# Attention and expert layer in one kernel: squares of the first two key blocks summed by VectorE, loads and splits of the first expert weights tied to later jobs, token operands of two chunks made by GpSimd

## The chip, the cores and the metric

The kernel runs on one core of a Trainium2 chip. The metric is the device time of one execution in microseconds (us). The engines are PE (TensorE), DVE (VectorE), ACT (ScalarE), POOL (GpSimd) and SP (SyncE, which only issues DMAs here). Each engine takes its own instructions in order and waits on semaphores for the others.

## What is computed

Random-feature attention, and on its result a mixture of eight experts, all in float32:

```python
proj = einsum('bhsd,md->bhsm', x, omega); sq = sum(x*x, -1) / 2   # x = q or k, scaled
phi  = exp(h - max(h)) / sqrt(m),  h = proj - sq
num  = phi(q) @ (phi(k)^T v);  den = phi(q) @ sum_s phi(k)        # B 4, H 8, S 576, D 64, m 128
x    = (num / (den + 1e-6)) as [2304, 512]
P    = exp(x @ w_gate - max), 8 rounds of row and column scaling
out += P[:, e:e+1] * (relu(x @ w1[e]) @ w2[e])                     # 8 experts, 512 -> 1024 -> 512
```

## The kernel before

**Attention, 36 jobs.** A job is one half (four heads, two rows of each partition) of a block of k or q; job 4 and job 21 are the leftover k rows ("kr"), 22 and 35 the leftover q rows ("qr"). Jobs 0 to 3 are k, from 5 on k and q take turns, from 31 on only q. A block of 512 KB serves two jobs that follow each other (0 and 1, 2 and 3; from job 5 on every second one, such as 5 and 7).

Each block is loaded (`load`) and its squares are summed (`squares`, L281): ACT squares 1024 numbers a partition into `sq`, POOL halves them three times (L290), DVE sums the last eight of each row (L292, `sqs`). Each job (`feature_stages`, L304) transposes on PE (L311, `tp`), copies to `th` (ACT for k, DVE for q), multiplies with omega (L324, `pp`), and DVE takes two maxima (L327, `mx`), the small shift `cn` (L331, L332: two inputs in SBUF) and `ex`; ACT does the exponentials (L339, L342). A k job then adds to `kv` on PE; a q job transposes, multiplies with `kvs`, and its result goes to `xf`.

**Operands.** When six token tiles of `xf` are complete (a chunk; three in all: chunk 0 is complete as job 21 begins, chunk 1 at job 34, chunk 2 after the last job), `token_operands` (L99) makes seven operand tiles: up to one DVE subtraction each on `xf` (L110, four in all), an ACT cast (L125), a DVE subtraction (L126), and a 768 KB store (L128). There are four `xs` buffers for all of it; chunk 2's tiles are used by the first matmuls (L539) straight away.

**Expert weights.** `stage` (L170) loads 1 MB of w1 or w2 in two DMAs of 512 KB to `st`, `split` (L180) makes one of seven high and low parts: up to one POOL operation on `st` or `t` (L186), an ACT cast `wh` (L216), and for the first w1 a POOL subtraction `wl` (L217). After the attention 16 units of 1/16 of the expert weights run, bound by matmuls.

**What sets the order.** The Python loop over the jobs (L740) names what may be done when, but a scheduler that plays the program through with a timeline of its own then sets each engine's order: what has no dependency is drawn forward. So the loads of `st`, written at jobs 6 and 24, stand on SP between the first loads of q and k. DMAs are numbered round eight semaphores, so that one waits for the eighth before it.

Of the kernel before, what the change touches and what calls it, by code (L numbers as in the profile page):

```python
# [9 lines left out]
F32 = mybir.dt.float32  # L10
F32R = mybir.dt.float32r
AF = mybir.ActivationFunctionType
ALU = mybir.AluOpType
# [3 lines left out]
def raw(ap):  # L17

    return ap.bitcast(F32)
# [3 lines left out]
def moe_attention_kernel(  # L23
# [23 lines left out]
    nc = tc.nc  # L47
    B, H, S, D = q.shape
# [4 lines left out]
    P = 128  # L53
# [26 lines left out]
    def bank(name):  # L80
        return ps[0].tile([P, 512], F32, tag="b", name=name)
# [9 lines left out]
    ORDER = [1, 5, 6, 3, 7, 2, 4]  # L91
# [4 lines left out]
    def token_tile():  # L96
        return xs.tile([P, 2, 2, HL], F32R, tag="xs", bufs=XSB, name="xs")

    def token_operands(c, x):  # L99

        def q(r, h):
            h = 1 - h
            return x[:, 2 * r : 2 * r + 2, h * HL : (h + 1) * HL]

        last = c == NCH - 1
        gate_steps = logits(c, x)
        next(gate_steps)

        def sub(o, a, b):
            nc.vector.tensor_tensor(o, a, b, op=ALU.subtract)  # L110

        for i in ORDER:
            if i == 5:
                sub(q(0, 0), q(0, 1), q(0, 0))
            elif i == 6:
                sub(q(0, 0), q(1, 1), q(0, 0))
            elif i == 7:
                sub(q(0, 1), q(1, 1), q(0, 1))  # L120
            elif i == 4:
                sub(q(0, 0), q(1, 0), q(0, 0))
            o = {3: q(1, 1), 7: q(0, 1), 2: q(1, 0)}.get(i, q(0, 0))
            t = token_tile()
            nc.scalar.copy(t[:, 0], o)  # L125
            nc.vector.tensor_tensor(t[:, 1], o, raw(t[:, 0]), op=ALU.subtract)  # L126
            xdram[c, i] = xd.tile([P, 2, 2, HL], F32, name=f"xd{c}_{i}")
            nc.sync.dma_start(out=xdram[c, i], in_=raw(t))  # L128
            if last:
                xop[0, c, i] = t  # L130
                first(0, c, i, 0)
                first(0, c, i, 1)
            next(gate_steps, None)
            yield
# [31 lines left out]
    wst, wt = {}, {}  # L166
    tmp = {}

    def stage(u, w):
        e, fb = units[u]  # L170
        f0 = fb * FB * P
        for r in range(2):
            wst[u, w, r] = t = wp.tile([P, 2, 2, HD], F32, tag="st", bufs=4, name="st")
            if w == 1:
                src = w1[e][r * HD : (r + 1) * HD, f0 : f0 + FB * P]
            else:
                src = w2[e][f0 + r * HD : f0 + (r + 1) * HD, :]
            nc.sync.dma_start(out=t.rearrange("p k h c -> p k (h c)"), in_=src.rearrange("(k p) c -> p k c", p=P))

    def split(u, w, i):  # L180

        def q(r, h):
            return wst[u, w, r][:, :, 1 - h if w == 1 else h]

        def tt(o, a, b, op=ALU.subtract):
            nc.gpsimd.tensor_tensor(o, a, b, op=op)  # L186


        if w == 1:

            if i == 5:
                tmp[u] = wp.tile([P, 2, HD], F32, tag="t", bufs=1, name="t")
                tt(tmp[u], q(0, 1), q(1, 1), ALU.add)
            elif i == 6:
                tt(tmp[u], tmp[u], q(0, 0))
            elif i == 3:
                tt(tmp[u], q(1, 0), tmp[u])
            elif i == 7:
                tt(q(0, 1), q(0, 0), q(0, 1))
            o = {1: q(0, 0), 7: q(0, 1), 2: q(1, 0), 4: q(1, 1)}[i] if i not in (5, 6, 3) else tmp[u]  # L200
        else:

            if i == 5:
                tt(q(0, 0), q(0, 1), q(0, 0))
            elif i == 6:
                tt(q(0, 0), q(0, 0), q(1, 1))
            elif i == 7:
                tt(q(0, 1), q(1, 1), q(0, 1))
            elif i == 4:
                tt(q(0, 0), q(1, 0), q(0, 0), ALU.add)  # L210
            o = {3: q(1, 1), 7: q(0, 1), 2: q(1, 0)}.get(i, q(0, 0))
        pool = wp if w == 1 else op_
        bufs = 7 * w
        hi = pool.tile([P, 2, HD], F32R, tag=f"w{w}h", bufs=bufs, name="wh")
        lo = pool.tile([P, 2, HD], F32R, tag=f"w{w}l", bufs=bufs, name="wl")
        nc.scalar.copy(hi, o)  # L216
        (nc.vector if u > 0 or (w == 2 and i in (1, 6, 7, 4)) else nc.gpsimd).tensor_tensor(lo, o, raw(hi), op=ALU.subtract)  # L217
        wt[u, w, i] = (hi, lo)
# [3 lines left out]
    sc = sc_cm.__enter__()  # L222
# [54 lines left out]
    sqt = {}  # L277
# [3 lines left out]
    def squares(which, key):  # L281

        t = rawt[which, key]
        n = 1 if key[0] == "r" else 2
        s = sc.tile([P, H, n, D], F32, tag="sq", bufs=2, name="sq")
        nc.scalar.activation(s, t[:, :H], AF.Square, scale=1.0 / math.sqrt(2.0 * math.sqrt(D)))
        w = D
        while w > 8:
            w //= 2
            nc.gpsimd.tensor_tensor(s[..., :w], s[..., :w], s[..., w : 2 * w], op=ALU.add)  # L290
        o = sc.tile([P, H, n], F32, tag="sqs", bufs=6, name="sqs")
        nc.vector.tensor_reduce(o, s[..., :w], axis=AX.X, op=ALU.add)  # L292
        sqt[which, key] = o

# [9 lines left out]
    def feature_stages(which, key, hh, on_act):  # L304


        tin = rawt[which, key].rearrange("p h j d -> p (h j d)")
        tp = bank("tp")
        for i in range(4):
            o = (4 * hh + i) * P  # L310
            nc.tensor.transpose(tp[:, i * P : (i + 1) * P], tin[:, o : o + P], ident)  # L311
        th = sc.tile([P, 4, P], F32, tag="th", bufs=2, name="th")
        if which == "k":
            nc.scalar.copy(th.rearrange("p a s -> p (a s)"), tp)
        else:
            nc.vector.tensor_copy(th.rearrange("p a s -> p (a s)"), tp)
        yield
        sq = sqt[which, key].rearrange("p h j -> p (h j)")
        mx = sc.tile([P, 4, 2], F32, tag="mx", bufs=4, name="mx")
        pp = [bank("pp") for _ in range(2)]  # L320
        for i in range(4):
            for g in range(2):
                r = slice(g * D, (g + 1) * D)
                nc.tensor.matmul(pp[g][:, i * M : (i + 1) * M], lhsT=th[r, i], rhs=omt[r], start=True, stop=True)  # L324
        p3 = [p.rearrange("p (h m) -> p h m", h=4) for p in pp]
        for g in range(2):
            nc.vector.reduce_max(mx[:, :, g], p3[g], axis=AX.X)  # L327

        s8 = sq[:, 8 * hh : 8 * hh + 8]
        cn = sc.tile([P, 8], F32, tag="cn", bufs=4, name="cn")  # L330
        nc.vector.tensor_tensor(cn, s8, mx.rearrange("p h g -> p (h g)"), op=ALU.subtract)  # L331
        nc.vector.tensor_tensor(cn, cn, s8, op=ALU.subtract)  # L332
        res = []
        for g in range(2):
            ex = sc.tile([P, 4, M], F32, tag="ex", bufs=8, name="ex")
            c4 = cn[:, g::2]
            if on_act and g == 1:
                for i in range(4):
                    nc.scalar.activation(ex[:, i, :], p3[g][:, i, :], AF.Exp, bias=c4[:, i : i + 1])  # L339
            else:  # L340
                nc.vector.tensor_tensor(ex, p3[g], c4.unsqueeze(2).to_broadcast([P, 4, M]), op=ALU.add)
                nc.scalar.activation(ex, ex, AF.Exp)  # L342
            res.append(ex)
        yield
        yield
        return res
# [369 lines left out]

    def ensure_loads(i):
        for it in list(need):
            if it[0] <= (i if it[1] == "v" else i + 2):
                need.remove(it)  # L720
                load(it[1], it[2])
                if it[1] != "v":
                    sq_todo.append(it)
        while sq_todo and sq_todo[0][0] <= i + 1:
            _, w, key = sq_todo.pop(0)
            squares(w, key)

    sq_todo = []
    active = []

    def tick():
        for it in list(active):
            jb, gen = it
            try:
                next(gen)
            except StopIteration:
                active.remove(it)

    ensure_loads(0)
    for i, jb in enumerate(jobs):  # L740
        if i == 4:
            prepare_gate()
        if i == 6:
            stage(0, 1)
        if i >= 8 and i % 2 == 0 and (i - 8) // 2 < 7:
            split(0, 1, ORDER[(i - 8) // 2])
        if i == 24:
            stage(0, 2)
        gen = k_job(jb[1], jb[2]) if jb[0] == "k" else q_job(*jb[1:])
        active.append((jb, gen))  # L750
        tick()
        ensure_loads(i + 1)
# [90 lines left out]
```

## Time and profile before

| | us |
|---|---|
| three runs: median (lowest to highest) | 1651.64 (1648.07 to 1652.31) |
| the profiled execution: its time, its span | 1651.03, 1649.1 |
| PE busy | 1589.7 (96%) |
| DVE, ACT, POOL busy | 1397.0, 778.0, 272.2 |

The profiled execution lies 0.61 us below the median and has 1.9 us around its span. A busy PE is not PE at its best: PE, DVE and ACT can each be busy while another sets the pace.

### The profile page before, as it was taken

Reading aid. Unit: us, or ns where it says so; the run is one execution under the profiler, and the core shown is the slowest. Engines: PE = TensorE matmul, PEld = TensorE weight load, DVE = VectorE, ACT = ScalarE, POOL = GpSimd, SP = SyncE. Lnnn points to the kernel's source line nnn. Section 1 sums busy time; section 2 is a strip of 40 time slices with the busy share of each in tenths; the row PEclk is TensorE's granted clock in tenths of the full one; section 3 lists DMA queues with packets and bytes.
Section 4 is the critical chain, followed back from the end, with each engine's and each line's share of the span. In section 5 each row is a group of like instructions: output and inputs, shape, how many; then the busy total and the mean of one; then the engine's idle time right before and its main releaser. Section 6 shows DMA issues by size and latency. Waiting matters only on the chain.

```text
span 1649.1 us, 31431 instructions
## 1 busy us (share of the span) xinstructions
PE 1589.7 (96%) x12318; PEld 1555.0 (94%) x12318; DVE 1397.0 (85%) x2771; ACT 778.0 (47%) x1396; POOL 272.2 (17%) x236
## 2 busy tenths in 40 slices
PE   5898889999999999999999999999999999999998
PEld 4777689999999999999999999999999999999997
DVE  4698889898979898889888898989898888889877
ACT  5687755444434343443544443444444444444333
POOL 6421041111102011111111110102111111101003
PEclk8799999999999999999999999999999999999999
DMA  9332576665665656566657565665665665655562
GB/s 232 110 110 110 213 284 234 204 229 170 237 201 200 216 200 212 202 218 217 218 177 257 168 220 202 216 210 206 210 217 207 217 216 185 218 185 192 175 227 78
DMA packets 105314, 329.79 MB, mean 200 GB/s; under 512 B 14800, under 2 KB 43984, under 8 KB 105168
## 3 DMA queue, kind: packets, MB, share of 16 engines
q1 hardware_dynamic: 105168, 327.79, 58.4%
q8 instruction: 98, 1.61, 0.4%
q14 instruction: 48, 0.39, 0.1%
HBM read 306.53 MB, written 21.23 MB: 199 GB/s over the span
## 4 chain that ended last, share of the span: by engine, by line
PE 83%; DVE 10%; POOL 2%; DMA 1%; issue 1%; ACT 1%; SPq 1%; DVEq 0%; ACTq 0%; POOLq 0%
PE hx L539 23%; PE x L640 22%; PE hz L539 17%; PE z L640 11%; PE w L640 5%; PE pp L324 2%; DVE out L666 2%; DVE sm L576 2%; DVE mx L327 1%; DVE bl L576 1%; POOL sq L290 1%; DVE wl L217 1%; PE np L425 1%; PE kv L351 1%; DVE sl L615 1%
## 5 line engine op out<-in xcount | busy, mean ns | idle before, releaser
L539 PE MATMUL hx<-xs,wh 128*128 128x384 f32 x1536 | 374.0, 337 | 1.9 <-ACT xs L125 1.3
L666 DVE SCALAR_TENSOR_TENSOR out<-x,prob,out 128x256 f32<-128x256 f32 x497 | 233.6, 476 | 65.6 <-PE x L640 64.2
L539 PE MATMUL hz<-xs,wh 128*128 128x384 f32 x1152 | 281.8, 336 | 1.7 <-ACT xs L125 1.0
L539 PEld LDWEIGHTS hx<-xs,wh 128*128 128x128 f32 x1536 | 269.7, 188 | 3.7 <-ACT xs L125 2.4
L186 POOL TENSOR_TENSOR st<-st 128x512 f32<-128x512 f32 x80 | 132.0, 1651 | 728.0 <-DVE wl L217 725.4
L539 PEld LDWEIGHTS hz<-xs,wh 128*128 128x128 f32 x1152 | 202.2, 188 | 3.2 <-ACT xs L125 1.8
L539 PE MATMUL hx<-xs,wl 128*128 128x384 f32 x768 | 199.2, 336 | 0.0
L618 ACT ACTIVATE bh<-hr 128x512 fp32r<-128x512 f32 x144 | 91.2, 634 | 222.8 <-PE x L640 217.9
L666 DVE SCALAR_TENSOR_TENSOR out<-z,prob,out 128x256 f32<-128x256 f32 x252 | 120.2, 477 | 57.9 <-PE z L640 57.1
L216 ACT CAST wh<-st 128x512 fp32r<-128x512 f32 x176 | 104.7, 620 | 110.6 <-PE hx L539 45.1
L614 ACT CAST sh<-sm 128x512 fp32r<-128x512 f32 x144 | 89.7, 623 | 139.3 <-PE z L640 99.7
L539 PE MATMUL hz<-xs,wl 128*128 128x384 f32 x576 | 150.1, 335 | 0.0
L539 PEld LDWEIGHTS hx<-xs,wl 128*128 128x128 f32 x768 | 138.7, 188 | 0.0
L576 DVE SCALAR_TENSOR_TENSOR sm<-hr,sm 128x256 f32<-128x256 f32 x288 | 133.7, 464 | 2.7
L217 DVE TENSOR_TENSOR wl<-st,wh 128x512 fp32r<-128x512 f32 x169 | 119.6, 719 | 13.1 <-ACT wh L216 12.8
L576 DVE SCALAR_TENSOR_TENSOR bl<-hr,bh 128x512 fp32r<-128x512 f32 x144 | 118.5, 823 | 2.5 <-ACT bh L618 2.5
L640 PE MATMUL z<-wh,sh 128*128 128x256 f32 x576 | 117.9, 281 | 2.8 <-ACT sh L597 2.7
L640 PE MATMUL x<-wh,sh 128*128 128x256 f32 x576 | 117.6, 284 | 0.7 <-DVE out L666 0.6
L640 PE MATMUL x<-wl,sh 128*128 128x256 f32 x576 | 118.3, 281 | 0.0
L588 ACT ACTIVATE ah<-hr 128x256 fp32r<-128x256 f32 x144 | 60.3, 419 | 122.1 <-PE x L640 98.9
L640 PE MATMUL z<-wh,sl 128*128 128x256 f32 x576 | 115.5, 282 | 1.6 <-DVE sl L598 1.6
L640 PE MATMUL z<-wl,sh 128*128 128x256 f32 x576 | 116.8, 281 | 0.0
(150 smaller groups left out, 3470.1 us busy)
## 6 DMA issues: line engine op xcount, KB each, us to landing
xs<-xd SPq DMA_DIRECT2D x329, 768.0 KB, 4.4
st<-in_moe_w_dram SPq DMA_DIRECT2D x64, 512.0 KB, 4.9
xd<-xs SPq DMA_DIRECT2D x21, 768.0 KB, 4.6
k<-in_k_dram SPq DMA_DIRECT2D x8, 512.0 KB, 4.8
v<-in_v_dram SPq DMA_DIRECT2D x8, 512.0 KB, 5.4
q<-in_q_dram SPq DMA_DIRECT2D x8, 512.0 KB, 4.2
out_dram<-out SPq DMA_DIRECT2D x32, 128.0 KB, 1.9
kr<-in_k_dram SPq DMA_DIRECT2D x4, 128.0 KB, 5.4
```

The costliest lines, as they stand in the source:

```text
L186: nc.gpsimd.tensor_tensor(o, a, b, op=op)
L216: nc.scalar.copy(hi, o)
L217: (nc.vector if u > 0 or (w == 2 and i in (1, 6, 7, 4)) else nc.gpsimd).tensor_tensor(lo, o, raw(hi), op=ALU.subtract)
L290: nc.gpsimd.tensor_tensor(s[..., :w], s[..., :w], s[..., w : 2 * w], op=ALU.add)
L324: nc.tensor.matmul(pp[g][:, i * M : (i + 1) * M], lhsT=th[r, i], rhs=omt[r], start=True, stop=True)
L539: nc.tensor.matmul(pb, lhsT=a[:, k, g * P : (g + 1) * P], rhs=x[:, b, k, :], start=i in (1, 5, 2) and j == 0, stop=j == len(prods) - 1, sk ...
L576: nc.vector.scalar_tensor_tensor(o, in0=a, scalar=0.0, in1=b, op0=ALU.max, op1=op)
L588: nc.scalar.activation(ah, a11, AF.Relu)
L614: nc.scalar.copy(sh, sm)
L618: nc.scalar.activation(bh, a[:, 1:], AF.Relu)
L640: nc.tensor.matmul(pb, lhsT=ops[s][i][a][:, f], rhs=wt[u, 2, i][b][:, f], start=bool(start) and j == 0, stop=j == len(prods) - 1, skip_gro ...
L666: nc.vector.scalar_tensor_tensor(o, in0=pb, scalar=p, in1=o, op0=ALU.mult, op1=ALU.add)
```

## The change

Six edits. (1) The first two blocks' squares (k of jobs 0 to 3) are no longer halved by POOL: DVE sums all 64 of each row. (2) `th` of those jobs is copied by DVE and not ACT. (3) Before the loads of the first w1 and w2, POOL copies eight numbers of the newest `cn` into the buffer, so that the load waits for that job. (4) The first w1 is loaded at job 10 and split from job 14 on. (5) Loads of k and q are named three jobs ahead (two before), squares two ahead (one before), with eight `sqs` buffers. (6) Both subtractions of an operand go to POOL for chunks 0 and 1.

```diff
+        eng = nc.vector if last else nc.gpsimd
         def sub(o, a, b):
-            nc.vector.tensor_tensor(o, a, b, op=ALU.subtract)
+            eng.tensor_tensor(o, a, b, op=ALU.subtract)
...
-            nc.vector.tensor_tensor(t[:, 1], o, raw(t[:, 0]), op=ALU.subtract)
+            eng.tensor_tensor(t[:, 1], o, raw(t[:, 0]), op=ALU.subtract)
...
             wst[u, w, r] = t = wp.tile([P, 2, 2, HD], F32, tag="st", bufs=4, name="st")
+            if u == 0:
+                nc.gpsimd.tensor_copy(t[:, 0, 0, :8], last_cn[-1])
...
-        while w > 8:
+        early = len(sqt) < 2
+        while w > 8 and not early:
...
-        if which == "k":
+        if which == "k" and len(sqt) > 4:
             nc.scalar.copy(th.rearrange("p a s -> p (a s)"), tp)
...
-            if it[0] <= (i if it[1] == "v" else i + 2):
+            if it[0] <= (i if it[1] == "v" else i + 3):
...
-        while sq_todo and sq_todo[0][0] <= i + 1:
+        while sq_todo and sq_todo[0][0] <= i + 2:
...
-        if i == 6:
+        if i == 10:
             stage(0, 1)
-        if i >= 8 and i % 2 == 0 and (i - 8) // 2 < 7:
-            split(0, 1, ORDER[(i - 8) // 2])
+        if i >= 14 and i % 2 == 0 and (i - 14) // 2 < 7:
+            split(0, 1, ORDER[(i - 14) // 2])
```

On DVE, before, job 3 (its maxima are `mx_283`) and job 4 (`mx_340`); `sqs_483` and `sqs_562` are the sums of the k block of jobs 9 and 11 and the q block of jobs 10 and 12:

```order
L327 TENSOR_REDUCE mx_283<-pp_285 128x4
L331 TENSOR_TENSOR cn_296<-sqs_122,mx_283 128x8
L332 TENSOR_TENSOR cn_296<-cn_296,sqs_122 128x8
L341 TENSOR_TENSOR ex_299<-pp_284,cn_296 128x512
L292 TENSOR_REDUCE sqs_483<-sq_478 128x16
L292 TENSOR_REDUCE sqs_562<-sq_557 128x16
L327 TENSOR_REDUCE mx_340<-pp_341 128x4
```

The same place in the changed kernel, where job 3's maxima are `mx_284`, job 4's `mx_334`, and the sums of those two blocks `sqs_421` and `sqs_480`:

```order
L349 TENSOR_TENSOR ex_237<-pp_222,cn_234 128x512
L299 TENSOR_REDUCE sqs_421<-sq_416 128x16
L299 TENSOR_REDUCE sqs_480<-sq_475 128x16
L334 TENSOR_REDUCE mx_284<-pp_285 128x4
L334 TENSOR_REDUCE mx_284<-pp_286 128x4
L338 TENSOR_TENSOR cn_297<-sqs_109,mx_284 128x8
L339 TENSOR_TENSOR cn_297<-cn_297,sqs_109 128x8
L349 TENSOR_TENSOR ex_300<-pp_285,cn_297 128x512
L299 TENSOR_REDUCE sqs_682<-sq_677 128x16
L299 TENSOR_REDUCE sqs_734<-sq_729 128x16
L334 TENSOR_REDUCE mx_334<-pp_335 128x4
```

Both pairs of sums now stand one job earlier; further on the sum for the k block of jobs 17 and 19 moves from in front of job 8's maxima to job 7's, and the three after it (a q block, kr, qr) all stand in front of job 9's.

On ACT in the changed kernel, from job 8's second exponential (`ex_580`) to job 10's (`ex_714`); `wh` are the casts of the first w1, which stood between jobs 1 and 4 before:

```order
L350 ACTIVATE ex_580<-ex_580 128x512
L292 ACTIVATE sq_1288<-qr_1231 128x512
L222 CAST wh_867<-st_597 128x512
L222 CAST wh_1014<-t_1012 128x512
L415 COPY qt_689<-qp_684 128x512
L347 ACTIVATE ex_663<-pp_646,cn_657 128x128 x4
L415 COPY qt_696<-qp_691 128x512
L350 ACTIVATE ex_660<-ex_660 128x512
L222 CAST wh_1148<-t_1012 128x512
L321 COPY th_727<-tp_722 128x512
L347 ACTIVATE ex_717<-pp_700,cn_711 128x128 x4
L350 ACTIVATE ex_714<-ex_714 128x512
```

Two casts now stand in front of job 9's exponentials and a third in front of job 11's `th`; the other four follow before job 11's exponentials.

On POOL in the changed kernel, chunk 0's operands (`xs`, `xf`), with the two copies that hold the load of the first w2:

```order
L128 TENSOR_TENSOR xs<-xf,xs 128x768
L112 TENSOR_TENSOR xf<-xf 128x2x384 x2
L128 TENSOR_TENSOR xs<-xf,xs 128x768
L179 COPY st<-cn 128x8 x2
L112 TENSOR_TENSOR xf<-xf 128x2x384
L372 TENSOR_TENSOR kvs<-kvs 128x4 x2
L128 TENSOR_TENSOR xs<-xf,xs 128x768 x3
L112 TENSOR_TENSOR xf<-xf 128x2x384
L128 TENSOR_TENSOR xs<-xf,xs 128x768
L192 TENSOR_TENSOR t<-st 128x512
L128 TENSOR_TENSOR xs<-xf,xs 128x768
L192 TENSOR_TENSOR st<-st 128x2x256
```

These eleven `xs` and `xf` subtractions stood on DVE between jobs 20 and 24; chunk 1's eleven moved in the same way.

## Rows read from the trace of the kernel before

**Rows 1.** Busy time by stage: PE, PEld, DVE, ACT, POOL, clock, DMA share, GB/s.

```profile
0.00:20.00 20.00, 10.31 (x96) 8.21 (x97) 6.44 (x14) 9.82 (x17) 11.39 (x26) 1.00 1.00 249
80.00:110.00 30.00, 28.42 (x504) 25.43 (x503) 27.56 (x73) 25.59 (x63) 10.10 (x15) 1.00 0.33 91
110.00:135.00 25.00, 21.67 (x322) 17.65 (x317) 23.02 (x51) 20.25 (x47) 3.38 (x5) 0.93 0.60 228
245.00:1649.00 1404.00, 1391.59 (x9847) 1383.51 (x9845) 1214.22 (x2377) 615.34 (x1033) 190.67 (x126) 1.00 0.60 204
```

**Rows 2.** Waits of DVE, 0 to 80 us: total, times, longest.

```profile
DVE sqs L292 <- POOL sq L290: 27.0, 8, 9.4
```

**Rows 3.** Timeline, DVE and POOL: start, length, what, idle before.

```profile
37.09 0.29 DVE L292 TENSOR_REDUCE sqs<-sq 128x16 f32<-128x128 f32 x1 [6.65 <-POOL sq L290]
38.93 1.28 DVE L327 TENSOR_REDUCE mx<-pp 128x4 f32<-128x512 f32 x2
...
47.37 1.28 DVE L327 TENSOR_REDUCE mx<-pp 128x4 f32<-128x512 f32 x2
95.55 2.64 POOL L290 TENSOR_TENSOR sq<-sq 128x512 f32<-128x512 f32 x3 [8.14 <-ACT sq L286]
```

**Rows 4.** Timeline, early loads on SP and a square.

```profile
13.96 2.25 SPq L178 DMA_DIRECT2D st<-in_moe_w_dram  x2
18.01 6.20 SPq L263 DMA_DIRECT2D qr<-in_q_dram  x2
24.32 0.56 SPq L274 DMA_DIRECT2D k<-in_k_dram  x1
30.44 1.06 ACT L286 ACTIVATE sq<-k 128x1024 f32<-128x1024 f32 x1 [3.02 <-DMA k<-in_k_dram]
```

**Rows 5.** Timeline, DVE's small `cn` beside POOL, and without.

```profile
22.59 0.93 DVE L331 TENSOR_TENSOR cn<-sqs,mx 128x8 f32<-128x8 f32 x1
23.46 1.26 POOL L186 TENSOR_TENSOR t<-st 128x512 f32<-128x512 f32 x1
23.56 1.18 DVE L332 TENSOR_TENSOR cn<-cn,sqs 128x8 f32<-128x8 f32 x1
29.34 0.17 DVE L331 TENSOR_TENSOR cn<-sqs,mx 128x8 f32<-128x8 f32 x1
```

**Rows 6.** Timeline, one k block from its load to its sum, and job 9.

```profile
52.65 0.37 SPq L274 DMA_DIRECT2D k<-in_k_dram  x1
56.66 1.06 ACT L286 ACTIVATE sq<-k 128x1024 f32<-128x1024 f32 x1 [1.31 <-DMA k<-in_k_dram]
61.10 0.27 DVE L292 TENSOR_REDUCE sqs<-sq 128x16 f32<-128x128 f32 x1
67.76 1.28 DVE L327 TENSOR_REDUCE mx<-pp 128x4 f32<-128x512 f32 x2
```

**Rows 7.** Timeline, a cast of the first w1 on ACT.

```profile
24.75 0.62 ACT L216 CAST wh<-t 128x512 fp32r<-128x512 f32 x1 [2.60 <-POOL t L186]
```

**Rows 8.** Groups to 245 us: count, busy, mean ns, idle before.

```profile
L126 DVE TENSOR_TENSOR xs<-xf,xs 128x768 fp32r<-128x768 f32 x21 | 19.7, 952 | 6.1 <-ACT xs L125 5.9
L125 ACT CAST xs<-xf 128x768 fp32r<-128x768 f32 x21 | 17.1, 840 | 4.6 <-DMA xd<-xs 2.6 <-DVE xf L110 1.7 <-DVE xs L126 0.3
L110 DVE TENSOR_TENSOR xf<-xf 128x768 f32<-128x768 f32 x12 | 11.4, 950 | 0.0
L290 POOL TENSOR_TENSOR sq<-sq 128x256 f32<-128x256 f32 x20 | 14.5, 728 | 2.0 <-ACT sq L286 1.3
L217 POOL TENSOR_TENSOR wl<-t,wh 128x512 fp32r<-128x512 f32 x3 | 3.8, 1266 | 0.0
```

**Rows 9.** Timeline, maxima of jobs 13, 20 and 24.

```profile
83.47 1.29 DVE L327 TENSOR_REDUCE mx<-pp 128x4 f32<-128x512 f32 x2 [0.38 <-PE pp L324]
107.98 1.29 DVE L327 TENSOR_REDUCE mx<-pp 128x4 f32<-128x512 f32 x2
131.70 1.28 DVE L327 TENSOR_REDUCE mx<-pp 128x4 f32<-128x512 f32 x2
```

**Rows 10.** Timeline, stores of chunks 1 and 2 on SP.

```profile
175.88 32.20 SPq L128 DMA_DIRECT2D xd<-xs  x14
```

More of the change, by code (lines that the diff above doesn't have):

```diff
@@ L167, in moe_attention_kernel @@
     tmp = {}
+    last_cn = []
     def stage(u, w):
@@ L287, in squares @@
         w = D
-        while w > 8:
+        early = len(sqt) < 2
+        while w > 8 and not early:
             w //= 2
             nc.gpsimd.tensor_tensor(s[..., :w], s[..., :w], s[..., w : 2 * w], op=ALU.add)
-        o = sc.tile([P, H, n], F32, tag="sqs", bufs=6, name="sqs")
+        o = sc.tile([P, H, n], F32, tag="sqs", bufs=8, name="sqs")
         nc.vector.tensor_reduce(o, s[..., :w], axis=AX.X, op=ALU.add)
@@ L332, in feature_stages @@
         nc.vector.tensor_tensor(cn, cn, s8, op=ALU.subtract)
+        last_cn.append(cn)
         res = []
```

## The prediction, made before the changed kernel ran

> **What bounds the kernel now.** I read the table of stages first. From 245 us to the end PE is busy for 1391.6 of 1404 us at full clock [rows 1]. The change touches nothing there but the order, so it has to win or lose in the first 245 us. In the first 20 us PE is busy for 10.3 us and DVE for 6.4; from 80 to 110 us PE, DVE and ACT are all busy for 85 to 95% [rows 1]. So the start is slack, and the middle is balanced between three engines.
>
> The waits of DVE come second: to 80 us it stood 27.0 us in front of `sqs`, waiting for POOL's halvings, 9.4 us of it before the first [rows 2]; 17.6 us are left that an edit could win. The timeline shows where: at 37.09 a sum waited 6.65 us, and job 4's maxima began at 38.93, job 5's at 47.37 [rows 3], against one job every 3.50 us in the middle (job 13 at 83.47, job 20 at 107.98, seven jobs) [rows 9]. Third, from 107.98 to 131.70 four jobs took 23.7 us and not 14.0 [rows 9]: chunk 0's operands stand on DVE, which is busy for 23.0 of 25 us there, but ACT for 20.3 too [rows 1].
>
> **Part 1, the start: squares, copies, earlier loads, weights out of the way.** Removed: six halvings and 1 MB of w1 and 1 MB of w2 among the early loads [rows 4], and eleven POOL operations of the first w1 (seven `wl`, four on `t` and `st`) of 1.26 us [rows 5, 8], 14 us of POOL between 22 and 52 us. Added on DVE: two sums of 1024 numbers for two of 128. A maximum pair reads 1024 numbers in 1.28 us [rows 3], so 1.3 for each, and four copies; DVE has room.
>
> What is late next is the loads, since the sums of later blocks stand one job earlier in DVE's order and DVE takes them in order. The k block of jobs 9 and 11 was issued at 24.32, behind `qr`, whose issue took 6.20 us [rows 4], and its square began at 30.44 after waiting for the DMA. 1 MB less ahead of it at 249 GB/s [rows 1] is 4 us: I take 26.4. Its square and q's take 1.06 us each, both chains on POOL 2 x 2.64 [rows 3, 4]: the second sum is ready at about 33, and now job 3's maxima wait for it. The next two blocks follow on POOL in 5.3 us, so job 4's maxima begin at about 38, hardly before the 38.93 of now. Job 5's no longer wait for a sum: one job on, with PE slow, about 41 for 47.37, a gain of 6.4.
>
> Half of that is lost at once. The k block of jobs 17 and 19 can load only when job 7's transposes free its buffer: issue at 52.65, sum at 61.10, 8.4 us later [rows 6]. That sum stood in front of job 8's maxima and now stands in front of job 7's, so job 8 gains one job (3.5 us) less than the 6: about 2.5. The three sums after it stand in front of job 9's maxima, now at 67.76 [rows 6], and pass POOL in order behind the two copies that hold `st`; I put job 9 at 65. So the start yields -3 us, with ends of -9 (loads land 6 us earlier, none of the sums waits) and +2 (the early waits cost more than the gain).
>
> **Part 2, the first w1 in the balanced stage.** ACT gets seven casts of 0.62 us [rows 7], 4.3 us, between jobs 9 and 12, and they are in order: the first waits for the load of `st`, which now starts only when job 8's `cn` exists and takes some 4 us from issue to use like the k block above (52.65 to 56.66) [rows 6]; the second waits for a `wl` and an operation on `t` on POOL, 2.5 us, as the one at 24.75 waited 2.60 [rows 7]. Behind them stand job 9's exponentials, then job 11's `th`, and PE waits for both. ACT is busy for 25.6 of 30 us [rows 1], so some 0.5 us a job can be made up. Also, POOL's eleven operations hold DVE's `cn`: 0.93 and 1.18 us beside POOL where it is 0.17 alone, 1.8 us a job [rows 5]. 4.3 + 2.5 + up to 4 of the load's wait, less what ACT has spare over four jobs and what overlaps the late DVE: +5 us. Ends: 0, if job 9 is late for its own reasons and covers it, and +9, if ACT's 6.8 us and one job's `cn` on each add up. Cover gone, this part eats all of part 1.
>
> **Part 3, chunk 0 on POOL.** Removed from DVE: 11 operations of 0.95 us, 10.5 us [rows 8], of the 9.7 us by which the four jobs exceed their pace. Added on POOL: 11 operations on 768 numbers. POOL takes 0.73 us for 256 and 1.27 for 512 [rows 8], so 1.8 us for 768 (an estimate on that line), 20 us in all, over about five jobs. Each job's two `cn` can be held: 1.8 us a job at 1.26 us an operation, so 2.6 at 1.8, and 13 us over five jobs if every one is hit; with none, 0. ACT keeps its seven casts of 0.84 (5.9 us) and sets a floor near its 20.3 us of 25. Ends: -9.7 and +3.5. I take -3, since the rows nearest to it (back-to-back POOL work) show both `cn` held.
>
> The Trainium skill states the same thing as a rule ("SBUF — State Buffer", section "Who interferes with whom"): a DVE operation with two inputs in SBUF contends with a GpSimd operation that reads SBUF, and whichever starts first keeps the port for its whole instruction. The trace agrees, with 0.93 and 1.18 us for a `cn` of 0.17 [rows 5]. By that rule alone, with every `cn` hit, this part is +3.5 us, and it is the mechanism of rival B below.
>
> **Part 4, chunk 1 on POOL and the end of the attention.** DVE loses another 10.5 us after job 33, so the last q jobs end sooner and chunk 2 can start earlier. But the last two chunks' 14 stores follow each other for 32.2 us [rows 10] through four buffers, and chunk 2's tiles need those that chunk 1 gives back. Chunk 1 takes 20 us on POOL and its last tile comes no earlier than now. DVE's own two-input subtractions for chunk 2 then meet POOL's. I take 0, with ends of -3 (the last q jobs set it) and +5 (POOL's and DVE's operations in turn: five of them by 0.95). The 1 MB of w2 has long landed either way, and the rest of the weights wait as before.
>
> **Sum.** -3 + 5 - 3 + 0 = -1 us on the profiled execution's 1651.03: 1650.0, which is 1650.6 beside the median of 1651.64. Forecast: no change, 1650 us.
>
> **Rivals.**
> A, the start carries through (faster). DVE's 17.6 us of waits [rows 2] do go: loads land early enough that job 9 is 8 us ahead; the casts find ACT idle, since the jobs are ahead of their loads, and cost 2; chunk 0 gives back 6 of its 9.7; the end gives 2. -8 + 2 - 6 - 2 = -14: 1637. For it: POOL is freed of 14 us just where DVE waits for it. Against it: the sums stand one job earlier, and the k block's 8.4 us from issue to sum [rows 6] does not shrink.
> B, the port shared by POOL and DVE (slower). In every stage to which POOL work is moved, two `cn` a job meet it: part 2 at its +9, chunk 0 at +3.5, the end at +3, the start -3: +12.5, 1663. It decides from the point where more than about three jobs in four have both `cn` held in chunks 0 and 1 and in w1's splits. For it: rows 5. Against: POOL waits for casts between its operations, and DVE has slack in some jobs.
> C, the change doesn't do what it says: the loads of `st` are tied, but SP takes DMAs in order and the qr issue still blocks behind full queues, so that the k block lands at 30.4 as before and job 3 waits until 37. Then the start is +2 or worse and the sum is +4: 1655, still no change.
>
> **How the numbers follow.** Less than 0.3%, 5 us, can't be told from no change here. No change (with C) has 0.42, its own range 1646 to 1656; A 0.35; B 0.23. The four parts' ends are independent of each other in the main, and make some 10 us either way (11, 9, 13 and 8 us from end to end; half of each squared, summed, and the root taken is 10.4). From 1650 I take 1638 below, which takes in nearly all of A, and 1659 above; about 0.1 is left out on each side.
>
> **What would show it.** In the changed profile: job 3's maxima at about 33 us and job 4's near 38 (part 1 right; at 25 and 29, A); a wait of DVE for POOL in front of job 7's maxima; job 9's maxima at 65. ACT's first cast of `wh` waiting for the DMA, its second for POOL, and job 13's maxima after 83.5, at some 85.5 (part 2). Mean `cn` well over 0.27 us between jobs 21 and 26, and jobs 20 to 24 in about 21 us (part 3). Fourteen stores in 30 to 34 us (part 4), PE busy 99% from there to the end. I am wrong if job 13 comes before 77 us or after 92, or if the stage after the attention shifts by more than 5 us through the new order of matmuls alone.

## The result and the profile after

| | before | after |
|---|---|---|
| median of runs side by side (lowest to highest), us | 1649.98 (1648.07 to 1652.31), 4 | 1661.59 (1658.41 to 1663.32), 4 |
| profiled execution: time, span, us | 1651.03, 1649.1 | 1658.41, 1656.6 |
| POOL busy, us | 272.2 | 308.0 |

The changed kernel is slower: ratio 1.0068, 95% interval 1.0045 to 1.009, 11.6 us more, where 1650 and no change were forecast; it lies above the forecast's upper end of 1659. The profiled execution is the fastest of its four (the others took 1661.35 to 1663.32 at a mean granted clock of 0.983 to 0.985, it 0.989), so the two profiles differ by only 7.4 us. That much can be followed row by row; the other 4 can't, and why the other three took longer stays open.

The last three stages of [rows 1], after (columns as there). From 245 us on PE is busy for 1398.0 of 1411 us, 99.1% as before, so what is lost is lost ahead of it. From 80 to 110 us PE and DVE have lost 2.5 and 1.7 us of work; POOL has almost five times as much as before from 110 to 135 (16.65 us for 3.38).

```profile
80.00:110.00 30.00, 25.90 (x442) 22.91 (x443) 25.90 (x65) 24.42 (x61) 12.56 (x19) 1.00 0.28 80
110.00:135.00 25.00, 22.03 (x319) 18.20 (x318) 21.48 (x42) 18.70 (x44) 16.65 (x15) 1.00 0.60 185
245.00:1656.00 1411.00, 1397.99 (x9888) 1389.28 (x9886) 1219.80 (x2385) 619.48 (x1042) 192.92 (x127) 1.00 0.60 204
```

DVE's waits to 80 us, after, as [rows 2]: those for POOL fell from 27.0 to 18.5 us, and 8.3 came for ACT, in front of the two long sums: 26.8 together, so hardly less.

```profile
DVE sqs L299 <- POOL sq L297: 18.5, 7, 7.5
DVE sqs L299 <- ACT sq L292: 8.3, 2, 6.7
```

DVE's timeline after, the sums that waited and the maxima behind them (jobs 3, 4, 7, 9, 13, 16 and 20 in this order). In [rows 3, 6, 9] jobs 4, 9, 13 and 20 stood at 38.93, 67.76, 83.47 and 107.98. The same pattern comes four times (jobs 3, 7, 9 and 16): a sum waits for POOL, and the maxima behind it begin 0.1 to 0.2 us after its start (at job 3 after a second sum, at 32.72).

```profile
32.26 0.29 DVE L299 TENSOR_REDUCE sqs<-sq 128x16 f32<-128x128 f32 x1 [7.47 <-POOL sq L297]
32.92 1.28 DVE L334 TENSOR_REDUCE mx<-pp 128x4 f32<-128x512 f32 x2
38.64 1.28 DVE L334 TENSOR_REDUCE mx<-pp 128x4 f32<-128x512 f32 x2
...
53.42 0.29 DVE L299 TENSOR_REDUCE sqs<-sq 128x16 f32<-128x128 f32 x1 [6.62 <-POOL sq L297]
53.63 1.28 DVE L334 TENSOR_REDUCE mx<-pp 128x4 f32<-128x512 f32 x2
...
65.46 0.22 DVE L299 TENSOR_REDUCE sqs<-sq 128x8 f32<-128x64 f32 x1 [1.32 <-POOL sq L297]
65.60 1.28 DVE L334 TENSOR_REDUCE mx<-pp 128x4 f32<-128x512 f32 x2
...
86.63 1.29 DVE L334 TENSOR_REDUCE mx<-pp 128x4 f32<-128x512 f32 x2
...
98.35 0.29 DVE L299 TENSOR_REDUCE sqs<-sq 128x16 f32<-128x128 f32 x1 [1.82 <-POOL sq L297]
98.55 1.28 DVE L334 TENSOR_REDUCE mx<-pp 128x4 f32<-128x512 f32 x2
...
113.10 1.29 DVE L334 TENSOR_REDUCE mx<-pp 128x4 f32<-128x512 f32 x2 [0.31 <-PE pp L331]
```

Job 7 shows the whole chain. Its transposes (`tp`) ended at 44.94 and freed the buffer for the k block of jobs 17 and 19, which was loaded at 45.00; job 7's own products (`pp`) were done at 48.32, but its maxima stand behind that block's sum, so they began at 53.63. PE and SP after:

```profile
44.28 0.66 PE L318 MATMUL tp<-ident,k 128*128 128x128 f32 x4
45.00 0.37 SPq L280 DMA_DIRECT2D k<-in_k_dram  x1
47.16 1.16 PE L331 MATMUL pp<-omt,th 64*128 64x128 f32 x16
```

ACT's first two casts of the first w1, after (the kind of [rows 7]):

```profile
66.30 0.62 ACT L222 CAST wh<-st 128x512 fp32r<-128x512 f32 x1 [2.60 <-DMA st<-in_moe_w_dram]
69.56 0.62 ACT L222 CAST wh<-t 128x512 fp32r<-128x512 f32 x1 [2.65 <-POOL t L192]
```

SP after, the end of the attention, which answers to [rows 10]: thirteen stores, the first reload of token operands (`xs<-xd`), the fourteenth store. Before, fourteen stores began at 175.88 and the first reload stood at 208.18.

```profile
182.01 32.22 SPq L130 DMA_DIRECT2D xd<-xs  x13
214.88 0.36 SPq L517 DMA_DIRECT2D xs<-xd  x1
216.21 0.32 SPq L130 DMA_DIRECT2D xd<-xs  x1
```

Where the 7.4 us of the profiles came from, by marks in both (job = start of its maxima, reload = first `xs<-xd`): to job 9 -2.2; job 9 to 13 +5.3; 13 to 20 +2.0; 20 to 28 +0.4; 28 to 35 -0.4; job 35 to the first reload +1.5; the rest +0.8.

### The profile page after: what moved, and what is told of

It is laid out like the page before. It is cut to its first block, busy times and chain, and to the rows that moved or that the text cites. A ratio compares the mean times of both kernels' runs of the same rounds, so it can differ in the third digit from the quotient of the medians.

```text
span 1656.6 us, 31441 instructions
## 1 busy us (share of the span) xinstructions
PE 1590.8 (96%) x12318; PEld 1555.9 (94%) x12318; DVE 1400.7 (85%) x2753; ACT 776.9 (47%) x1392; POOL 308.0 (19%) x256
## 4 chain that ended last, share of the span: by engine, by line
PE 81%; DVE 11%; POOL 3%; DMA 2%; issue 2%; ACT 1%; SPq 0%; DVEq 0%; POOLq 0%; ACTq 0%
PE hx L547 23%; PE x L648 22%; PE hz L547 18%; PE z L648 11%; PE w L648 5%; DVE out L674 2%; DVE sm L584 2%; POOL sq L297 2%; DVE mx L334 1%; PE pp L331 1%; DVE bl L584 1%; DMA k<-in_k_dram 1%; DVE sl L623 1%; DVE cn L338 1%; DVE wl L223 1%
## 5 line engine op out<-in xcount | busy, mean ns | idle before, releaser
L674 DVE SCALAR_TENSOR_TENSOR out<-x,prob,out 128x256 f32<-128x256 f32 x497 | 233.3, 476 | 67.2 <-PE x L648 65.7
```

The source lines that it names most:

```text
L674: nc.vector.scalar_tensor_tensor(o, in0=pb, scalar=p, in1=o, op0=ALU.mult, op1=ALU.add)
```

## The experiments

All were timed beside the kernel before. Marks are from one profiled execution of each. "Sums ahead" counts the `sqs` that stand in DVE's queue in front of the maxima of jobs 7, 16 and 20.

| kernel | sums ahead | job 9 | 13 | 20 | 28 | 35 | reload | end | median, us | ratio (95%) |
|---|---|---|---|---|---|---|---|---|---|---|
| before | 9, 14, 16 | 67.8 | 83.5 | 108.0 | 148.6 | 176.7 | 208.2 | 1649.1 | 1649.98 | |
| after | 10, 16, 17 | 65.6 | 86.6 | 113.1 | 154.1 | 181.8 | 214.9 | 1656.6 | 1661.59 | 1.0068 (1.0045, 1.009) |
| x1_tokens_dve | 10, 16, 17 | 65.0 | 88.4 | 115.0 | 154.8 | 182.6 | 214.1 | 1655.3 | 1656.62 | 1.0034 (1.0021, 1.0048) |
| x2_chunk0_pool | 10, 16, 17 | 65.7 | 86.5 | 113.0 | 153.8 | 181.6 | 213.1 | 1655.1 | 1656.90 | 1.0043 (1.0031, 1.0056) |
| x3_before_tokens_pool | 9, 14, 16 | 65.8 | 80.0 | 104.4 | 146.8 | 175.9 | 212.7 | 1656.3 | 1658.56 | 1.0049 (1.0036, 1.0061) |
| x4_start_alone | 10, 16, 17 | 71.6 | 89.4 | 115.6 | 158.1 | 187.3 | 218.8 | 1658.2 | 1660.67 | 1.0062 (1.0049, 1.0075) |
| y1_staging_alone | 9, 14, 16 | 56.4 | 77.9 | 103.0 | 145.1 | 173.1 | 205.9 | 1651.1 | 1652.91 | 1.0016 (1.0005, 1.0027) |
| y2_old_lookahead | 10, 16, 17 | 66.9 | 90.2 | 116.4 | 157.2 | 184.9 | 218.8 | 1661.0 | 1659.08 | 1.0056 (1.0042, 1.007) |
| y3_start_no_look | 10, 16, 17 | 71.8 | 89.9 | 116.2 | 158.2 | 187.8 | 219.3 | 1660.4 | 1660.98 | 1.0071 (1.0058, 1.0084) |
| y4_lookahead_alone | 9, 14, 16 | 67.8 | 82.0 | 106.5 | 146.2 | 174.2 | 205.7 | 1647.4 | 1649.48 | 1.0001 (0.9991, 1.0011) |
| z3_bufs8 | 10, 16, 17 | 69.1 | 85.5 | 111.7 | 153.6 | 182.6 | 214.1 | 1654.5 | 1658.32 | 1.0051 (1.0037, 1.0064) |
| z7_start_bufs6 | 9, 14, 16 | 65.7 | 79.9 | 104.4 | 144.1 | 172.2 | 203.7 | 1644.1 | 1651.65 | 1.0009 (0.9997, 1.0022) |
| z4_after_bufs6 | 9, 14, 16 | 59.6 | 81.4 | 106.4 | 145.9 | 173.6 | 207.5 | 1648.6 | 1650.43 | 0.9999 (0.9989, 1.0009) |
| z6_after_bufs6_chunk0 | 9, 14, 16 | 58.6 | 81.3 | 106.0 | 145.3 | 173.1 | 204.6 | 1649.4 | 1649.87 | 0.9998 (0.999, 1.0007) |
| w7_after_seven | 10, 15, 17 | 65.2 | 90.3 | 115.0 | 156.0 | 183.7 | 217.5 | 1658.4 | 1657.69 | 1.0051 (1.0036, 1.0066) |
| w_before_4 | 7, 12, 14 | 61.8 | 76.4 | 100.8 | 141.4 | 169.5 | 201.0 | 1642.8 | 1643.21 | 0.9958 (0.9945, 0.9971) |
| w_tok_4 | 7, 12, 14 | 52.7 | 78.3 | 102.7 | 143.0 | 172.1 | 203.6 | 1647.8 | 1652.16 | 1.0011 (1.0001, 1.002) |
| w_tok_5 | 8, 13, 15 | 55.7 | 81.9 | 106.3 | 147.2 | 175.3 | 206.8 | 1648.0 | 1650.43 | 1.0002 (0.9993, 1.001) |
| v4_chunk0 | 7, 12, 14 | 59.4 | 73.9 | 98.4 | 137.9 | 166.0 | 197.5 | 1639.6 | 1642.59 | 0.9961 (0.9946, 0.9976) |
| v4_start | 7, 12, 14 | 64.1 | 78.7 | 103.0 | 146.1 | 174.1 | 205.6 | 1648.4 | 1645.22 | 0.9974 (0.9963, 0.9984) |

One further execution of w7_after_seven took 3115 us and is left out of its median.

**First set: which part?** Theory S was a sum of small losses, T the chunks on GpSimd, M the matmul order and the clock.

```diff
 x1: -        eng = nc.vector if last else nc.gpsimd
     +        eng = nc.vector
 x2: +        eng = nc.gpsimd if c == 0 else nc.vector
 x3: (before) + edit 6 alone
 x4: (before) + edits 1, 2 and 5 alone
```

x1_tokens_dve. 

> The changed kernel with chunks 0 and 1 back on VectorE (the other edits stay). Theory S (a sum of small losses, each in its place: +3.2 us by job 13 from the early squares and the moved splits, +1.8 at job 16 where a sum now stands one job earlier in VectorE's order, about nothing from chunk 0, +2 to 3 from chunk 1): job 13's maxima at 86.6 us as in the changed kernel, job 28's at 153 to 154, the first store of chunk 1 at about 181, but the last store some 2 us earlier than the changed kernel's 216; 1658 to 1660. Theory T (all of the loss is the token chunks on GpSimd, and what comes before is caught up again): 1650 to 1652. Theory M (the matmul order after the attention and the clock make the difference, not the attention): the attention ends when it did, within 1 us, and the total moves freely.

x2_chunk0_pool. 

> The changed kernel with only chunk 0 on GpSimd, chunk 1 on VectorE. Theory S: jobs 20 to 28 as in the changed kernel (113, 154 us), chunk 2's first subtraction on VectorE no longer stretched from 0.95 to 2.41 us, the last store some 2 to 3 us earlier than 216; 1658 to 1660, within 1 us of the variant with both on VectorE. Theory T: half of the loss, 1655 to 1657. Theory M: moves freely.

x3_before_tokens_pool. 

> The kernel before, with chunks 0 and 1 on GpSimd and nothing else. Theory S: job 20 at 108 us as before, job 24 some 2 us before 131.7, job 26 with nothing left of it, the last store 2 to 3 us after 208; 1652 to 1653. Theory T: 1660 to 1662.

x4_start_alone. 

> The kernel before, with the first two sums and the first copies on VectorE and the loads and squares one job further ahead; the first weights' loads and splits stay where they were. Theory S: jobs 3 to 9 earlier than before, at most 3 us at job 9, job 16 with a wait for its sum, job 20 within 2 us of 108; 1648 to 1651. Theory T (the start is caught up in any case): 1650. If the lookahead alone is the loss: job 20 at 110 to 113 and 1653 to 1655.

None of the three theories held. With the token chunks back on DVE, 6 to 7 us of loss remain (T falls). The start alone costs 11.1 us, the tokens alone 9.0, all of it together 11.6: the parts don't add up (S falls in this form). The time after the first reload is 1439.4 to 1443.6 us in all of these, 1440.9 before: M explains at most 2.7 us, in x3. What x1 and x2 do show is that chunk 0 on POOL is worth nothing in time, and that chunk 1 on POOL costs 4.7 (medians of after and x2).

**Second set: which part of the start?** Theory L was the lookahead, theory W the moved splits.

```diff
 y1: (before) + edits 3 and 4 alone
 y2: (after)  -else i + 3   +else i + 2     -<= i + 2:   +<= i + 1:
 y3: (before) + edits 1 and 2 alone, and sqs bufs=8 of edit 5
 y4: (before) -else i + 2   +else i + 3     -<= i + 1:   +<= i + 2:
```

y1_staging_alone. 

> The kernel before, with nothing but the first weights' loads tied to a cn, staged from job 10 and split from job 14 on. Theory L (what costs ahead of job 20 is the lookahead: a sum stands one job earlier in VectorE's order while its load can come no sooner): the loads at the start get earlier and no sum is brought forward; jobs 5 and 9 earlier than in the kernel before by 3 to 6 us, some 3 to 5 of it lost between jobs 9 and 13; job 20 at 106 to 109 us; 1647 to 1651. Theory W (the moved splits are what costs): job 13 at 86 us or later, job 20 at 112; 1655 to 1657.

y2_old_lookahead. 

> The changed kernel with the lookahead of the kernel before (loads two jobs ahead, squares one). Theory L: no wait of 6 us ahead of job 7, none ahead of job 16; job 20 at 107 to 110 us (113.1 in the changed kernel), the first reload of token operands at 210 to 212 us instead of 214.9; 1655 to 1658. Theory W: job 20 at 112 or later, no better than 1660.

y3_start_no_look. 

> The kernel before, with only the first two sums and the first copies moved to VectorE. Theory L: jobs 3 to 5 come earlier by 1 to 4 us and the rest as before, job 20 at 105 to 108; 1647 to 1650. Theory W, or any by which the early sums themselves cost: 1652 or more.

y4_lookahead_alone. 

> The kernel before, with only the loads three jobs ahead and the squares two. Theory L: as with the whole start alone, waits for sums ahead of jobs 4, 6, 7 and 9 that add up, job 20 at 112 to 116 us; 1655 to 1661. Theory W: within 2 us of 1650.

Theory L fell on both sides: the lookahead alone changes neither the count of sums ahead nor the time (1649.48), and taking it out of the changed kernel leaves the wait ahead of job 7 (7.25 us) and 1659.08. W fell too: the moved splits alone cost 3 us, and in y1's profile job 20 is 5 us early; its rest after the first reload takes 1445.2, so some 4 us are lost behind the attention there; whether by the order of the matmuls was not tried. What costs 11 us is y3. But why should two sums on DVE do that? The column "sums ahead" is the same in all the slow starts, and what y3, x4 and the change share besides the sums and copies is one number, `bufs=8` of `sqs`. It belongs to edit 5, its line is not among those of the diff shown for the change, and what was expected of x4 and y3 does not name it.

**Third set: eight buffers.** Theory Q puts the loss on the buffers, theory E on the early sums and copies.

```diff
 z3: (before) -tag="sqs", bufs=6   +tag="sqs", bufs=8
 z7: (before) + edits 1 and 2, sqs left at bufs=6
 z4: (after)  -tag="sqs", bufs=8   +tag="sqs", bufs=6
 z6: z4 and x2 together
```

z3_bufs8. 

> The kernel before, with eight buffers for sqs where it has six, and nothing else. Theory Q (the two extra buffers let each later sum be put one job earlier into VectorE's queue, where it waits for a load that comes no sooner, and the maxima wait behind it): waits for GpSimd's halvings ahead of jobs 7, 9, 16 and 21, job 20 at 112 to 116 us, 1655 to 1661. Theory E (the first two sums of 1024 and the copies are what costs, by the first 20 us or by what they do to the order): as the kernel before, within 2 us of 1650.

z7_start_bufs6. 

> The kernel before, with the first two sums and the first copies on VectorE, and sqs at its six buffers. Theory Q: the later sums stand where they stood, no wait of over 1 us ahead of jobs 16 and 21, job 20 at 105 to 109 us; 1646 to 1651. Theory E: as with eight buffers, job 20 at 114 to 116 us; 1658 to 1662.

z4_after_bufs6. 

> The changed kernel with six buffers for sqs and nothing else changed. Theory Q: the wait of 6.6 us ahead of job 7's maxima goes, as do those ahead of jobs 16 and 21; job 20 at 103 to 108 us where the changed kernel has 113; what chunk 1 on GpSimd costs stays; 1653 to 1657. Theory E: 1660 to 1662.

z6_after_bufs6_chunk0. 

> The changed kernel with six buffers for sqs, and chunk 1 back on VectorE (chunk 0 on GpSimd). Theory Q, with chunk 1 on GpSimd as the other cost (about 5 us): job 20 at 103 to 108, the stores of chunks 1 and 2 in 32 us, 1647 to 1652. Theory E: 1655 to 1658, as the changed kernel with chunk 1 on VectorE.

Q held and E fell, though two times lie just outside Q's ranges: z4 2.6 us below it, z7 0.65 above. Two more buffers, nothing else, make the kernel before 8.2 us slower; two fewer make the changed one 11.2 us faster, as fast as before. DVE in z3_bufs8, whose job 7 stood at 58.15 before:

```profile
59.76 0.29 DVE L292 TENSOR_REDUCE sqs<-sq 128x16 f32<-128x128 f32 x1 [6.27 <-POOL sq L290]
59.97 1.28 DVE L327 TENSOR_REDUCE mx<-pp 128x4 f32<-128x512 f32 x2
...
68.87 0.29 DVE L292 TENSOR_REDUCE sqs<-sq 128x16 f32<-128x128 f32 x1 [1.79 <-POOL sq L290]
```

The same place in z4_after_bufs6, jobs 7 to 9. The sum that ended at 53.7 in the changed kernel ends at 53.0 here, its k block being loaded at 44.66 (45.00 there); but job 7 no longer stands behind it, and by job 9 six us are gained:

```profile
48.20 1.29 DVE L334 TENSOR_REDUCE mx<-pp 128x4 f32<-128x512 f32 x2 [1.72 <-PE pp L331]
52.71 0.28 DVE L299 TENSOR_REDUCE sqs<-sq 128x16 f32<-128x128 f32 x1 [0.55 <-POOL sq L297]
52.91 1.28 DVE L334 TENSOR_REDUCE mx<-pp 128x4 f32<-128x512 f32 x2
58.33 0.29 DVE L299 TENSOR_REDUCE sqs<-sq 128x16 f32<-128x128 f32 x1 [2.94 <-POOL sq L297]
59.63 1.28 DVE L334 TENSOR_REDUCE mx<-pp 128x4 f32<-128x512 f32 x2
```

So the buffer count was the brake that kept the scheduler from drawing the sums forward: with six, the seventh sum can't be put ahead of the last use of the first. The column of sums ahead fits this in every kernel: by job 16 eight blocks have had their last job, and with 4, 5, 6, 7 and 8 buffers 12, 13, 14, 15 and 16 sums stand ahead of it. The loss of z3's profile is there before the expert layer: +5.9 us at the first reload, 1440.4 us behind it (1440.9 before). z7 spreads from 1645.88 to 1656.18 and can't be told from before.

**Fourth and fifth set: steps, and the other direction.**

```diff
 w7: (after)  -bufs=8  +bufs=7       w_before_4: (before) -bufs=6  +bufs=4
 w_tok_4, w_tok_5: x2 with bufs=4, 5
 v4_chunk0: w_before_4 + chunk 0 on POOL     v4_start: w_before_4 + edits 1 and 2
```

w7_after_seven. 

> The changed kernel with seven buffers for sqs. With seven, two sums stand ahead of job 9's maxima where eight put three and six put one, one stands ahead of job 7's as with eight, and from job 10 on the order is that of six. Theory Q: the wait ahead of job 7 (6 us) stays, that ahead of job 16 (1.8 us) goes: job 9 at 63 to 66, job 16 at 94 to 97 (98.55 with eight, 91.92 with six); 1653 to 1658, between the two. Theory O (something else that eight buffers change, or the order of the matmuls after the attention): no relation to the number; 1650 or 1661.

w_before_4. 

> The kernel before with four buffers for sqs: one sum fewer stands ahead of jobs 4 and 5. Theory Q: the waits for sums ahead of jobs 4 and 5 (1.35 and 4.05 us) shrink, job 5 at 42 to 45 us for 47.4, of which 0 to 3 us are left at job 20 (105 to 108), since the loads bound job 8 to 10 in any case; 1647 to 1651. Theory O, or buffers that come free too late: 1652 to 1656.

w_tok_4. 

> The changed kernel with four buffers for sqs, and chunk 1 back on VectorE. Theory Q: with the early weights out of the way and the sums late in the queue, job 5 at 38 to 40 and job 20 at 103 to 106 us, the first reload at 202 to 205; 1644 to 1650. If buffers come free too late ahead of jobs 28 and 29: 1650 to 1654.

w_tok_5. 

> The changed kernel with five buffers for sqs, and chunk 1 back on VectorE. Theory Q: as with four up to job 20, within 1 us; 1645 to 1650.

v4_chunk0. 

> The kernel before with four buffers for sqs and chunk 0 on GpSimd. If the gain of chunk 0 is given back (its last q block is loaded behind the stores of chunk 0 on SyncE, which wait for GpSimd's slower subtractions): jobs 20 to 24 in 20 to 21 us (24.3 with VectorE), job 28 no earlier than 140 (141.4 with VectorE), 1641 to 1646, no difference to four buffers alone (1643.2). If the gain stays: 3 us less, 1640. If GpSimd's chunk delays the q block: 1646 to 1650.

v4_start. 

> The kernel before with four buffers for sqs and the first two sums and the first copies on VectorE. Theory Q: job 4 at 33 us for 37.5, job 9 at 59 to 61 for 61.8, as the loads allow, job 20 within 2 us of 100; 1641 to 1646. If two sums ahead of job 5 cost what they save: 1646 to 1650.

Seven buffers lie between six and eight in time (1657.69), with the wait ahead of job 7 (7.09 us) and without that ahead of job 16. But its job 16 came at 101.2 and not at 94 to 97, because jobs 9 to 13 took 25.1 us: a miss in the place, and only half a proof of steps. The other direction is the strongest evidence: four buffers and nothing else make the kernel before 6.8 us faster, more than expected. DVE's waits in it to 135 us, where [rows 2] had 27.0 to 80 us (none is added there from 80 to 135), and job 5, 47.37 in [rows 3]:

```profile
DVE sqs L292 <- POOL sq L290: 19.8, 5, 9.5
```

```profile
42.05 0.28 DVE L292 TENSOR_REDUCE sqs<-sq 128x16 f32<-128x128 f32 x1
43.42 1.29 DVE L327 TENSOR_REDUCE mx<-pp 128x4 f32<-128x512 f32 x2 [1.09 <-PE pp L324]
```

In the changed kernel fewer than six gain nothing: with chunk 1 on DVE, six, five and four buffers take 1649.87, 1650.43 and 1652.16 us, the last two above the 1650 that theory Q allowed at most. In w_tok_4 job 9 comes at 52.7, 15 us before that of the kernel before, and 10 of them are gone by job 13 (25.6 us for four jobs, 15.7 before), where the moved splits stand. v4_chunk0 is no faster than w_before_4 in time (1642.59 and 1643.21). v4_start is no better in time, and its marks, from its slowest execution, miss theory Q's (job 9 at 64.1 for 59 to 61). No kernel tried is clearly faster than the one before with one number changed.

## Why the prediction was wrong

**What bounds the kernel** held: 6.7 of the profiles' 7.4 us are there when the first reload is issued.

**Which step failed.** By the marks of the two profiles the sum's -1 us came as +7.4: to job 9 -2.2 (predicted -3), jobs 9 to 13 +5.3 (+5), jobs 13 to 20 +2.0 (no term), jobs 20 to 28 +0.4 (-3), from there to the end +1.9 (0). So the step that failed most by these marks is Part 3's -3, a gain that did not come, and next is the stretch from job 13 to 20, which "So the start yields -3 us" let run as before. Under the start lies a cost that got no term of its own: the two extra `sqs` buffers. The other 4 us of the medians are in none of these marks.

**Part 1: the places were right, the sum behind them was not.** Job 3 came at 32.92 (33 predicted), job 4 at 38.64 (38), job 5 at 40.96 (41), the k block of jobs 17 and 19 took 8.4 us from its load at 45.00 to its sum at 53.42 (8.4), in front of job 7, and job 9 came at 65.60 (65). But two errors cancel at job 9, and that is luck: with six buffers the same start has it at 59.6, so the gain was 8.2 us and not 6.4, and the earlier place of the sums took 6.0 of it and not half of 6.4. Behind job 9 the buffers go on: job 16 waited 1.8 us for a sum that stands two places further ahead than before, and jobs 13 to 20 took 26.2 to 26.6 us in all seven kernels with eight buffers, 24.3 to 25.1 in all others. In medians the buffers cost 11.2 us in the changed kernel and 8.2 alone. Without them the change comes to 1650.43 us, which is near the 1650 of the forecast by luck too: its terms, in the order above, are -8.2, +6.1, +0.5, -1.1 and +2.2. I had read the rows of the order and seen every sum stand a job earlier, and took them for the work of the lookahead; in y4 the lookahead moves none and costs nothing.

**Part 2 held in this profile.** ACT's first cast waited 2.60 us for the DMA, the second 2.65 for POOL; jobs 9 to 13 took 5.3 us more than before (+5 predicted), 6.1 with six buffers, 5.8 in y1. Job 13 came at 86.6 (85.5). Over the ten kernels with the moved splits these four jobs took 20.8 to 26.2 us, 5.1 to 10.5 more than the 15.7 before, so +5 is at their lower end.

**Part 3 failed in size.** Jobs 20 to 24 took 21.7 us (21 predicted, 23.7 before), but job 25 followed 6.5 us later, and by job 28 the gain was gone: -3 was predicted, +0.4 came. The table bears this out: jobs 20 to 28 took 39.3 to 42.4 us in the ten kernels with chunk 0 on POOL and 39.7 to 43.1 in the ten without. The term that was too small is the held `cn`, priced at 0 to 13 us; the -3 leaves 6.7 for it. The reason given for -3, that rows show both `cn` held, doesn't lead to it: with both held the same sum gives +3.5. From job 21 to 25 eight of the ten were held, 11.6 us for the 1.4 that eight take alone; these 10.2 us are about what the subtractions that left DVE had taken, 10.5. It begins with one `cn` a job and ends with both. That the held `cn` alone made job 25 late is not shown: in y1, with chunk 0 on DVE, job 25 came 7.1 us after job 24. DVE after, jobs 21, 23 and 24:

```profile
120.42 1.81 DVE L338 TENSOR_TENSOR cn<-sqs,mx 128x8 f32<-128x8 f32 x1
...
131.05 1.34 DVE L338 TENSOR_TENSOR cn<-sqs,mx 128x8 f32<-128x8 f32 x1
132.43 1.73 DVE L339 TENSOR_TENSOR cn<-cn,sqs 128x8 f32<-128x8 f32 x1
...
136.18 1.53 DVE L338 TENSOR_TENSOR cn<-sqs,mx 128x8 f32<-128x8 f32 x1
137.75 1.73 DVE L339 TENSOR_TENSOR cn<-cn,sqs 128x8 f32<-128x8 f32 x1
```

POOL at the same time, 1.8 to 1.9 us for each subtraction, as estimated:

```profile
120.40 3.71 POOL L112 TENSOR_TENSOR xf<-xf 128x768 f32<-128x768 f32 x2
...
130.55 5.36 POOL L128 TENSOR_TENSOR xs<-xf,xs 128x768 fp32r<-128x768 f32 x3 [0.57 <-ACT xs L127]
```

A second link is a queue that I had not followed: on SP the load of the last q block, used from job 28 on, stands behind stores of chunk 0, which wait for POOL's subtractions. In the changed kernel it is not what set that load: SP's last wait before it, 1.1 us, is for PE's transposes, which free the buffer. SP after, and its waits from 130 to 142 us:

```profile
132.39 7.41 SPq L130 DMA_DIRECT2D xd<-xs  x4
141.02 0.39 SPq L280 DMA_DIRECT2D q<-in_q_dram  x1
```

```profile
SPq L130 <- POOL xs L128: 8.4, 4, 3.2
SPq L280 <- PE tp L318: 1.1, 1, 1.1
```

In x3 the queue does set it: there SP waits only for POOL in that stretch.

```profile
SPq L130 <- POOL xs L128: 6.6, 2, 3.4
```

Job 27 of x3 is 5.3 us ahead of the kernel before, but the q block is loaded at 133.94, only 2.9 us earlier than there, its square waits 2.36 us for the DMA and its sum 3.27 for POOL, and job 28 is 1.8 us ahead.

**Part 4** lay a little above: the fourteenth store left 34.5 us after the first (30 to 34 predicted), and the first reload came 1.5 us later after job 35 than before. In medians chunk 1 on POOL costs 4.7 us with eight buffers (after and x2) and 0.6 with six (z4 and z6), where z4's profile loses 3 us to the reload and has 3.7 back behind it. Between 0 and 5 this stays open, and x3 may mean more.

**The rivals.** B gave the time, 1663, but not the whole reason: with no token work on POOL (x1) some 60% of the loss is there, and with all of it on POOL and six buffers (z4) none. B is not refuted, though: in the kernel before, edit 6 alone costs 9.0 us (x3). Of the 7.2 us in x3's profile 5.3 come between job 35 and the first reload, and DVE stands 3.26 us there in front of an `hr` sum of the expert layer, which waits for PE, with three of chunk 2's subtractions behind it in its order:

```profile
203.07 0.95 DVE L128 TENSOR_TENSOR xs<-xf,xs 128x768 fp32r<-128x768 f32 x1
207.28 0.56 DVE L558 TENSOR_TENSOR hr<-hz,hr 128x384 f32<-128x384 f32 x1 [3.26 <-PE hz L541]
207.76 0.95 DVE L128 TENSOR_TENSOR xs<-xf,xs 128x768 fp32r<-128x768 f32 x1
```

In z4 the first `hr` sum (205.10) does not wait and has two behind it. That this is the reason was not tried; why edit 6 costs 9.0 us alone and nothing in z4 stays open. Of A, "job 9 is 8 us ahead" is what six buffers give. C did not come: job 3 began at 32.92 and not at 37.

The rule of the Trainium skill ("SBUF — State Buffer", section "Who interferes with whom") is borne out by the rows, and harder at the end than I had assumed: chunk 2's subtractions on DVE took 2.41 us for 0.95, and POOL's 2.57 for 1.82. DVE, then POOL, after:

```profile
196.16 2.41 DVE L128 TENSOR_TENSOR xs<-xf,xs 128x768 fp32r<-128x768 f32 x1 [2.58 <-POOL xs L128]
198.67 2.41 DVE L112 TENSOR_TENSOR xf<-xf 128x768 f32<-128x768 f32 x1
```

```profile
192.36 5.39 POOL L128 TENSOR_TENSOR xs<-xf,xs 128x768 fp32r<-128x768 f32 x3 [1.04 <-ACT xs L127]
197.70 2.57 POOL L112 TENSOR_TENSOR xf<-xf 128x768 f32<-128x768 f32 x1
```

In the time of the changed kernel with six buffers this is not seen; what it costs with eight stays open.

## What to carry to other kernels

Where a scheduler orders in-order engines, the number of buffers of a small tile is an ordering rule: more of them let its producer be drawn forward in the queue, and if the producer waits for a load that comes no sooner, everything behind it waits too. Price a changed buffer count as a move of every instruction that writes the tile, and try fewer buffers as well as more. And when an engine's work is moved to a slower one, follow its DMA queue to the next load behind the stores, and read which wait ends last there: in x3 it was the queue, in the changed kernel the buffer.

## What the runs showed of the hardware

Two executions of the same order differ more than I had thought: x3's DVE queue is that of the kernel before up to job 20, yet its job 11 stands at 72.6 and not at 76.1, its job 20 at 104.4 and not 108.0. From 70 to 80 us PE's granted clock was 1.00 in x3 and 0.83 in the kernel before. A single mark under 4 us says little; the medians decide.

PE's granted clock was lower where PE stood. From 40 to 60 us it stood behind job 7's sum in the changed kernel, and does not with six buffers; the two lines (columns as in [rows 1]) are of the changed kernel and of z4_after_bufs6:

```profile
40.00:60.00 20.00, 13.24 (x220) 11.45 (x220) 11.32 (x24) 11.62 (x29) 3.98 (x7) 0.83 0.34 93
```

```profile
40.00:60.00 20.00, 15.64 (x270) 13.24 (x266) 13.96 (x32) 13.84 (x35) 7.62 (x15) 1.00 0.38 103
```

At 0.83 the stretch is partly at the lower level of 1.2 GHz, at 1.00 all at 2.4. A `pp` matmul took 325 ns on average in the one and 283 in the other, so part of what stood around the wait ran slower too. The eight buffers are not alone in this: in the kernel before, which waited for sums at jobs 4 and 5, the clock of the same stretch was 0.57 and a `pp` matmul took 417 ns.
